# Top-k attention with a squared-ReLU feed-forward: reciprocals of the row sums moved from VectorE to GpSimd, ScalarE's step in another order

## The chip, the core and the metric

The kernel runs on one core of a Trainium2 chip. A core has five engines that run their own instruction streams in order and wait for each other by semaphores: TensorE (PE; its weight loads are listed apart as PEld), VectorE (DVE), ScalarE (ACT), GpSimd (POOL) and SyncE (SP, which here only issues DMAs). The metric is the device time of one execution in microseconds (us).

## What is computed

```python
# q, k, v: (8, 8, 576, 64) float32
scores = (1 / sqrt(64)) * q @ k^T                        # per batch and head, 576 x 576
kth = np.partition(scores, -32, axis=-1)[..., -32:-31]   # 32nd largest of each row
scores = np.where(scores >= kth, scores, -1e9)
attn = exp(scores - max(scores))
attn = attn / (sum(attn) + 1e-9)
x = concat_heads(attn @ v)                               # (4608, 512)
h = np.maximum(x @ w_in, 0.0)                            # w_in (512, 2048)
out = (h * h) @ w_out                                    # w_out (2048, 512)
```

The division by the row sum is the part that the change moves: for each row the kernel needs one reciprocal.

## The kernel before

The 64 pairs of batch and head are taken in twos (`pairs`, 32 of them), and the rows of a pair in chunks of 128. A step `u` (there are `U` = 144, listed in `steps`) handles two such blocks, x = 0 and 1, side by side: 128 rows against all 576 keys, twice. The main loop `for u in range(U)` is a software pipeline written out by hand; `pin` keeps the instructions of each engine in the order in which the program makes them. In one turn of the loop different parts belong to different steps:

- `scores(u + 1)`: TensorE multiplies q and k into two PSUM tiles, `sc_a` and `sc_b` (the two halves of the keys), and ScalarE copies them to SBUF as `s` (L266).
- `pairs_of`, `quads_of`, `both`, `lesser`, `copy_far`: maxima and minima of groups of four scores. VectorE makes the maxima (L282 to L292), GpSimd gets the lesser ones by integer sum and difference (L307, L316), ScalarE copies one tile for it (`most`, L298). The first `EARLY` = 20 steps use a narrower form.
- `topk(u)`: four rounds of VectorE's eight maxima (L342), with the found ones struck out between them (L346). The 32nd value is the bound of the row.
- `drop(u - 1)`: ScalarE negates the row's largest and 32nd value (`neg`, L361); GpSimd compares each score with the bound, once for each x (TENSOR_SCALAR into `gone`, L378), and the result is added to `s` so that dropped scores fall far below zero: by GpSimd itself in the first 20 steps (L380), later by a DMA that GpSimd issues and that adds as it writes (L382).
- `exps(u - 2)`: ScalarE's exponentials into `w_two` (L386); `turn(u - 2)`: SP issues the DMA transpose into `wT`.
- `products(u - 3)`: TensorE multiplies `wT` with v into the one PSUM tile `av_ps`. v carries a column of ones, so that column 64 of the result is the row sum.
- `finish(u - 4)`: `invert` takes the reciprocal of the row sums (`rsum`, VectorE, L436), and `place` multiplies by it on ScalarE while copying to `x_tok` (L452), or to `x_rem` for the steps that hold the last 64 rows of two heads (L459, four instructions instead of two).
- `dense(u, 0)`, `dense(u, 1)`: pieces of the feed-forward part for rows that are ready. An up piece is eight matmuls into a bank `gen`, followed by its `rest`: relu (`rl`, L538) and square (`h`, L544) on ScalarE. A down piece is four matmuls into `dn_ps`; the fourth of a block is followed by a copy (`wide`, L561) and the stores. With `later=True` the `rest` is kept in the list `behind` and run in the next step, behind `topk(u, (0,))` and ahead of `finish`.
- `prepare(u)`: one of the four units that get the next pair ready: q or k transposed by TensorE and copied by ScalarE (`main`, L162), the last rows (`rest`, L199 to L202), and v converted (`values`, L206 and L209). `due(i)` says from which step the units of pair `i` are taken up; `scores(u + 1)` forces what is still missing.
- `w_casts`: the weights converted to bf16 on ScalarE, one piece a step from step 3 on (L624).

So ScalarE's stream in a step of the middle reads: `neg`, the `rest` put off from the step before (relu, square), `x_tok` twice, two score copies, two exps, a preparation if there is one, `most`, v's casts or `wide` if there are any, and a relu and square of the first piece if that was an up piece. GpSimd's reads: two comparisons, the DMA issue, the integer sum, the integer difference.

Of the kernel before, what the change touches and what calls it, by code (L numbers as in the profile page):

```python
# [13 lines left out]
f32 = mybir.dt.float32  # L14
# [3 lines left out]
ALU = mybir.AluOpType  # L18
AF = mybir.ActivationFunctionType
# [4 lines left out]
def kernel(  # L24
# [9 lines left out]
    nc = tc.nc  # L34
# [10 lines left out]
    def pin(ins):  # L45
        tc.keep_in_program_order(ins)
        return ins

    const = ctx.enter_context(tc.tile_pool(name="const", bufs=1))
# [4 lines left out]
    small = fast.enter_context(tc.tile_pool(name="small", bufs=2))  # L54
# [36 lines left out]
    NP = len(pairs)  # L91
# [28 lines left out]
    def fetch(n):  # L120
        while n and fetches:
            fetches.pop(0)[1]()
            n -= 1
# [117 lines left out]
    U = len(steps)  # L241
# [58 lines left out]
    def both(u):  # L300
        d = st[u]
        d["cat"] = scp.tile([128, 2, S], f32, name="cat", bufs=2)
        n_h = 1 if u < EARLY else 2
        wide = n_h * QUAR
        s, less = d["s"], d["cat"][:, :, HALF:HALF + wide].bitcast(i32)
        tt = nc.gpsimd.tensor_tensor
        pin(tt(less, s[:, :, 0:wide].bitcast(i32), s[:, :, HALF:HALF + wide].bitcast(i32), op=ALU.add))  # L307
# [47 lines left out]
    def by_vector(u, x):  # L355
        return u == U - 1 or (u == U - 2 and x == 1)

    def negate(u, ends):
        neg = small.tile([128, 2, 2], f32, name="neg", bufs=4)
        got = st[u]["ends"] if ends == 2 else st[u]["ends"][:, :, 0:1]  # L360
        pin(nc.scalar.activation(neg[:, :, 0:ends], got, AF.Copy, scale=-1.0))  # L361
        return neg
# [7 lines left out]
                e = d["e"][x] = scp.tile([128, S], bf16, name="e", bufs=3)  # L370
                pin(nc.scalar.activation(e[:, :], d["s"][:, x, :], AF.Exp, bias=neg[:, x, 0:1]))

    def drop(u, x):
        d = st[u]
        if x == 0:
            d["neg"] = negate(u, 2)
        s, byte = d["s"], gone[u % 2]
        pin(nc.gpsimd.tensor_scalar(byte[:, x, :, 1], s[:, x, :], scalar1=d["neg"][:, x, 1:2], scalar2=-HUGE, op0=ALU.add, op1=ALU.mult))  # L378
        if by_vector(u, 1) or u < EARLY:
            pin(nc.gpsimd.tensor_tensor(s[:, x, :], s[:, x, :], byte[:, x, :, :].rearrange("p n two -> p (n two)").bitcast(bf16), op=ALU.add))  # L380
        elif x == 1:
            pin(nc.gpsimd.dma_start(out=s[:, :, :].rearrange("p x n -> p (x n)"), in_=byte[:, :, :, :].rearrange("p x n two -> p (x n two)").bitcast(bf16), accum_op=ALU.add))  # L382
# [44 lines left out]
    def sums(u):  # L427
        if u < U - 2:
            return av
        if not last_two:  # L430
            last_two["ps"] = ps_sc.tile([128, 2, 512], f32, name="sc_a")
        return last_two["ps"][:, u - (U - 2), 0:130].rearrange("p (x d) -> p x d", x=2)

    def invert(u):
        r = small.tile([128, 2, 1], f32, name="rsum", bufs=4)
        pin(nc.vector.reciprocal(r[:, :, :], sums(u)[:, :, 64:65]))  # L436
        st[u]["r"] = r

    x_tok = {}
# [4 lines left out]
    def place(u):  # L444
        for x, (i, c, a) in enumerate(steps[u]):
            b, pr = pairs[i]
            o, r = sums(u)[:, x, :], st[u]["r"]
            if c < 4:
                if (b, c) not in x_tok:
                    x_tok[b, c] = ffp.tile([128, 512], bf16, name="x_tok", bufs=8)  # L450
                h = 2 * pr + a
                pin(nc.scalar.activation(x_tok[b, c][:, h * 64:(h + 1) * 64], o[:, 0:64], AF.Copy, scale=r[:, x, :]))  # L452
                left[b, c] = left.get((b, c), 8) - 1
                if left[b, c] == 0:
                    full.append((b, c))
            else:
                for g in range(2):
                    h, rows = 2 * pr + g, slice(64 * g, 64 * g + 64)
                    pin(nc.scalar.activation(x_rem[b % 2][rows, h * 64:(h + 1) * 64], o[rows, 0:64], AF.Copy, scale=r[rows, x, :]))  # L459
                left[b, 4] = left.get((b, 4), 4) - 1  # L460
                if left[b, 4] == 0:
                    soon_moves.append(lambda b=b: rem_unit(b))
        del st[u]
# [35 lines left out]
    def rem_unit(b):  # L499
        tp = ps_one.tile([128, KH, 128], bf16, name="gen", bufs=2)  # L500
        for kh in range(KH):
            pin(nc.tensor.transpose(tp[:, kh, :], x_rem[b % 2][:, kh * 128:(kh + 1) * 128], id_h[:, :]))
        g = b // 2

        def rest():
            for a in range(2):
                rows = slice(64 * a, 64 * a + 64)
                pin(nc.scalar.activation(xt_rem[g % 2][rows, :, (b % 2) * 64:(b % 2 + 1) * 64], tp[rows, :, 64 * a:64 * a + 64], AF.Copy))
            if b % 2:
                rem = xt_rem[g % 2]  # L510
                stores = [[(slice(64 * a, 64 * a + 64), out[(b - 1 + a) * S + 512:(b + a) * S]) for a in range(2)]]
                block(lambda kh: rem[:, kh, :], stores)
        return rest
# [61 lines left out]
    behind = []  # L575

    def piece(later=False):
        turn_of[0] ^= 1
        for q_ in ((ups, downs), (downs, ups))[turn_of[0]]:
            if q_:  # L580
                rest = q_.pop(0)()
                if rest and later:
                    behind.append(rest)
                elif rest:
                    rest()
                return True
        return False

    def dense(u, x, later=False):
        for go in ripe.pop(u, ()):  # L590
            go()
        if moves and x == 1:
            rest = moves.pop(0)()
            if rest and later:
                behind.append(rest)
            elif rest:
                rest()
        if x == 1:
            moves.extend(soon_moves)
            soon_moves.clear()  # L600
        N = 2 if (u >= U - 14 and x == 0) or len(ups) + len(downs) > 24 else 1
        for n in range(N):
            if not piece(later and N == 1) and n == 0 and u < U:
                idle_piece()
# [28 lines left out]
    soon, coming = prep_units(0), 1  # L633
    soon.pop(0)()


    def due(i):
        return first[4 * (i // 4) + 3] - 1 - 4 * (3 - i % 4) if i >= 4 else first[i] - 1

    def prepare(u):  # L640
        nonlocal coming
        if not soon and coming < NP and u >= due(coming) - 4:
            assert coming < 5 or qk_left[coming - 5] == 0
            while fetches and fetches[0][0] <= coming:
                fetch(1)
            soon.extend(prep_units(coming))
            if coming + 1 < NP:
                load_pair(coming + 1)
            coming += 1
        if soon:  # L650
            soon.pop(0)()

    ones = const.tile([128, 1], f32, name="ones")
    pin(nc.gpsimd.memset(ones[:, :], 1.0))
    worst = const.tile([128, 1], f32, name="worst")
# [12 lines left out]
    def ok(w):  # L668
        return 0 <= w < U

    def finish(w):
        if ok(w):
            invert(w)
            place(w)
# [11 lines left out]
    for u in range(U):  # L686
        for x in range(2):
            if ok(u - 1) and not by_vector(u - 1, x):
                drop(u - 1, x)
        quads_of(u)  # L690
        topk(u, (0,))
        while behind:
            behind.pop(0)()
        finish(u - 4)
        if ok(u + 1):
            for i, c, a in steps[u + 1]:
                while coming <= i or (coming == i + 1 and soon):
                    prepare(u)
            scores(u + 1)
            both(u + 1)  # L700
        if ok(u - 2):
            exps(u - 2, 0)
            exps(u - 2, 1)
            turn(u - 2)
        fetch(10 if u < 8 else 3)
        casts_next = bool(soon) and soon[0].__name__ == "values"
        for _ in range(0 if casts_next else 2 if u < 8 else 1):
            prepare(u)
        if u >= Z:
            turn_x(u)  # L710
        topk(u, (1, 2))
        if ok(u + 1):
            pairs_of(u + 1)
            copy_far(u + 1)
            lesser(u + 1)
        topk(u, (3,))
        if casts_next:
            prepare(u)
        if by_vector(u, 1):
            early_exps(u)  # L720
        if u == U - 1:
            exps(u - 1, 0)
        dense(u, 0)
        dense(u, 1, later=8 <= u < U - 1)
        products(u - 3)
        turn_x(u)
        if w_casts and u >= 3:
            w_casts.pop(0)()
        if w_loads and u >= 1:
            w_loads.pop(0)()  # L730
# [163 lines left out]
```

## Time and profile before

| | us |
|---|---|
| Median of 3 runs | 951.43 (948.77 to 954.14) |
| The profiled execution, its own time | 953.31 |
| Its span | 951.5 |
| VectorE busy | 900.3 |
| ScalarE busy | 785.7 |
| GpSimd busy | 775.7 |
| TensorE busy (matmuls) | 690.8 |

In the profile a row of a group reads: line of the program, engine, operation, written tile `<-` read tiles, shapes, number of instructions; busy us and mean ns of one; and the time that the engine stood idle just before them, with what ended it. A row of the timeline reads: start us, duration us, engine, line, operation, tiles, number of merged instructions, and in brackets the idle time before and its releaser. Instructions of one engine overlap a little, so the step from one start to the next can be shorter than a duration.

### The profile page before, as it was taken

How to read it: one execution, taken by the hardware profiler on the slowest of the kernel's cores; microseconds unless marked ns; L12 is line 12 of the kernel's file. 1: busy time of each engine (PE TensorE's matmuls, PEld its weight loads, DVE VectorE, ACT ScalarE, POOL GpSimd, SP SyncE). 2: the span in 40 equal slices, each digit the busy share in tenths (PEclk: the TensorE clock that was granted, in tenths of full speed). 3: DMA queues.
4: the chain of work that ended last, by engine and by line, in shares of the span. 5: the costliest groups of instructions: out<-in, count | busy, mean ns of one | idle time of the engine just before them, and what ended most of it. 6: DMA issues, size and time to landing. Idle time of an engine off the chain costs nothing.

```text
span 951.5 us, 19120 instructions
## 1 busy us (share of the span) xinstructions
PE 690.8 (73%) x5264; PEld 424.4 (45%) x5264; DVE 900.3 (95%) x3635; ACT 785.7 (83%) x1778; POOL 775.7 (82%) x803
## 2 busy tenths in 40 slices
PE   6677767777767777777777777678677776777866
PEld 3333344444444445444444435444444443544544
DVE  5999999999999999999999999899999999899972
ACT  4677797898898879797998878788889877988982
POOL 7888888888888888888888888788888888788840
PEclk9898897988998998989899998987999899799999
DMA  5567766999997998989998899887999989977741
GB/s 138 118 168 160 169 129 132 192 186 208 185 211 160 198 214 185 203 163 197 197 211 177 189 211 171 199 173 166 206 186 200 193 194 203 176 166 164 154 94 43
DMA packets 329969, 166.17 MB, mean 175 GB/s; under 512 B 306560, under 2 KB 306560, under 8 KB 329856
## 3 DMA queue, kind: packets, MB, share of 16 engines
q1 hardware_dynamic: 311088, 92.62, 50.1%
q0 software_dynamic: 17568, 71.97, 33.0%
q8 instruction: 45, 0.74, 0.3%
q14 instruction: 68, 0.56, 0.2%
q10 hardware_dynamic: 1200, 0.30, 0.1%
HBM read 37.75 MB, written 9.44 MB: 50 GB/s over the span
## 4 chain that ended last, share of the span: by engine, by line
DVE 61%; ACT 15%; issue 11%; PE 7%; DMA 3%; SPq 1%; POOL 1%; ACTq 0%; POOLq 0%
DVE m L342 25%; DVE cat L346 16%; DVE sc_b L282 5%; ACT s L266 5%; DVE cat L291 5%; DVE cat L292 5%; DVE most L283 4%; ACT w_two_b L386 2%; PE gen L533 2%; ACT w_two_a L386 2%; PE dn_ps L556 1%; PE sc_a L263 1%; DVE rsum L436 1%; PE sc_b L263 1%; ACT x_tok L452 1%
## 5 line engine op out<-in xcount | busy, mean ns | idle before, releaser
L342 DVE MAX8 m<-cat 128x8 f32<-128x104 f32 (+3 forms) x1152 | 448.2, 432 | 0.0
L346 DVE MATCH_REPLACE8 cat<-m,cat 128x104 f32<-128x104 f32 (+2 forms) x864 | 271.8, 324 | 0.0
L307 POOL TENSOR_TENSOR cat<-s 128x576 int32<-128x576 int32 (+1 forms) x144 | 218.6, 1518 | 17.9 <-ACT s L266 17.0
L316 POOL TENSOR_TENSOR cat<-cat,most 128x576 int32<-128x576 int32 (+1 forms) x144 | 190.0, 1319 | 40.1 <-ACT most L298 24.1
L263 PE MATMUL sc_b<-qkT 64*128 64x288 f32 x512 | 109.1, 495 | 118.8 <-DVE cat L292 55.9
L533 PE MATMUL gen<-xT,w_in 128*128 128x256 bf16 (+1 forms) x1120 | 146.1, 282 | 34.0 <-ACT qkT L162 18.5
L533 PEld LDWEIGHTS <-w_in 128*128 128x128 bf16 x1408 | 127.2, 105 | 86.3 <-issue 56.4
L556 PE MATMUL dn_ps<-w_out,h 128*128 128x512 bf16 x576 | 161.9, 417 | 3.6 <-ACT wide L561 3.6
L263 PE MATMUL sc_a<-qkT 64*128 64x288 f32 x512 | 104.9, 474 | 53.2 <-DVE most L283 28.5
L263 PEld LDWEIGHTS sc_b<-qkT 64*128 64x128 f32 x512 | 49.4, 208 | 166.2 <-ACT neg L361 63.3
L378 POOL TENSOR_SCALAR gone_a<-s,neg 128x576 uint8<-128x576 f32 x143 | 106.7, 746 | 20.4 <-ACT neg L361 9.3
L378 POOL TENSOR_SCALAR gone_b<-s,neg 128x576 uint8<-128x576 f32 x142 | 105.9, 746 | 17.9 <-ACT neg L361 6.8
L452 ACT ACTIVATE x_tok<-av_ps,rsum 128x64 bf16<-128x64 f32 x252 | 64.9, 308 | 58.5 <-DVE rsum L436 58.3
L266 ACT ACTIVATE s<-sc_b 128x576 f32<-128x576 f32 x144 | 94.7, 657 | 7.5 <-PE sc_b L263 7.3
L266 ACT ACTIVATE s<-sc_a 128x576 f32<-128x576 f32 x144 | 93.7, 651 | 5.1 <-PE sc_a L263 4.4
L544 ACT ACTIVATE h<-rl 128x512 bf16<-128x512 f32 x138 | 87.0, 630 | 4.4
L538 ACT ACTIVATE rl<-gen 128x512 f32<-128x512 f32 x142 | 83.8, 590 | 8.0 <-PE gen L533 7.8
L556 PEld LDWEIGHTS <-h 128*128 128x128 bf16 x576 | 55.5, 105 | 70.8 <-issue 33.2
L422 PEld LDWEIGHTS <-wT 128*128 128x128 bf16 (+1 forms) x1600 | 66.4, 105 | 33.1 <-DMA wT<-w_two_c 7.4
L282 DVE TENSOR_TENSOR sc_b<-sc_a,s 128x288 f32<-128x288 f32 x144 | 66.3, 461 | 12.0 <-ACT s L266 9.9
L263 PEld LDWEIGHTS sc_a<-qkT 64*128 64x128 f32 x512 | 44.8, 197 | 65.4 <-ACT w_two_c L386 16.3
L386 ACT ACTIVATE w_two_a<-s,neg 128x576 bf16<-128x576 f32 x96 | 69.6, 783 | 1.8 <-DMA s<-gone_a 1.6
(165 smaller groups left out, 1227.2 us busy)
## 6 DMA issues: line engine op xcount, KB each, us to landing
s<-gone_a POOLq DMA_DIRECT2D x61, 576.0 KB, 4.7
s<-gone_b POOLq DMA_DIRECT2D x61, 576.0 KB, 4.8
v_raw<-in_v_dram SPq DMA_DIRECT2D x64, 128.0 KB, 3.1
out_dram<-wide SPq DMA_DIRECT2D x32, 256.0 KB, 2.7
k_raw<-in_k_dram SPq DMA_DIRECT2D x63, 128.0 KB, 3.1
q_raw<-in_q_dram SPq DMA_DIRECT2D x63, 128.0 KB, 3.3
wide<-in_moe_w_in_dram SPq DMA_DIRECT2D x8, 512.0 KB, 4.2
wide<-in_moe_w_out_dram SPq DMA_DIRECT2D x8, 512.0 KB, 4.0
```

Source lines behind the costliest of these rows:

```text
L263: pin(nc.tensor.matmul(out=ps[j][:, x, 0:HALF], lhsT=lhsT, rhs=rhs, start=True, stop=True))
L266: pin(nc.scalar.activation(s[:, :, j * HALF:(j + 1) * HALF], ps[j][:, :, 0:HALF], AF.Copy))
L282: pin(tt(far, one[:, :, QUAR:HALF], two[:, :, QUAR:HALF], op=ALU.max))
L307: pin(tt(less, s[:, :, 0:wide].bitcast(i32), s[:, :, HALF:HALF + wide].bitcast(i32), op=ALU.add))
L316: pin(tt(less, less, d["most"][:, 0:n_h, :, :].bitcast(i32).rearrange("p h x n -> p x h n"), op=ALU.subtract))
L342: pin(nc.vector.max(out=m[r][:, x, :], in_=part(r, x)))
L346: pin(nc.vector.match_replace(out=part(r, x), in_to_replace=m[r][:, x, :], in_values=part(r, x), imm_value=NEG))
L378: pin(nc.gpsimd.tensor_scalar(byte[:, x, :, 1], s[:, x, :], scalar1=d["neg"][:, x, 1:2], scalar2=-HUGE, op0=ALU.add, op1=ALU.mult))
L386: pin(nc.scalar.activation(w_two[u % 3][:, x, 0:S], d["s"][:, x, :], AF.Exp, bias=d["neg"][:, x, 0:1]))
L533: pin(nc.tensor.matmul(out=hp[:, n * n_rows:(n + 1) * n_rows], lhsT=w_in[:, kh, (f0 + n) * 128:(f0 + n + 1) * 128], rhs=xt(kh), start=(kh ...
L544: pin(nc.scalar.activation(h2, flat, AF.Square))
L556: pin(nc.tensor.matmul(out=op[:, :], lhsT=held["h2"][:, f, c * 128:(c + 1) * 128], rhs=w_out[:, f, :], start=(f == 0), stop=(f == NF - 1)))
```

## The change

Except in the last five steps, the reciprocal is no longer taken by VectorE from PSUM. ScalarE copies the two columns of sums to SBUF (`total`), and GpSimd raises them to the power of -1 with a tensor of minus ones as exponent. `invert(u - 4)` is called from within `drop(u - 1, 1)`, behind the comparison of x = 1 and ahead of the DMA issue (or of the addition, in the first 20 steps). `place(u - 4)` moves behind the score copies and the preparation of the step, and the preparation moves ahead of the exps. The `rest` of the second piece is not put off any more. For the last eight pairs `due` gives fixed steps. ScalarE's stream in a step then reads: `neg`, `total`, two score copies, a preparation, `x_tok` twice, two exps, `most`, casts or `wide`, relu and square. GpSimd's reads: two comparisons, the power, the DMA issue, the integer sum, the integer difference.

```diff
-    def drop(u, x):
+    def drop(u, x, between=None):
         d = st[u]
         if x == 0:
             d["neg"] = negate(u, 2)
         s, byte = d["s"], gone[u % 2]
         pin(nc.gpsimd.tensor_scalar(byte[:, x, :, 1], s[:, x, :], scalar1=d["neg"][:, x, 1:2], scalar2=-HUGE, op0=ALU.add, op1=ALU.mult))
+        if between:
+            between()
         if by_vector(u, 1) or u < EARLY:
...
     def invert(u):
         r = small.tile([128, 2, 1], f32, name="rsum", bufs=4)
-        pin(nc.vector.reciprocal(r[:, :, :], sums(u)[:, :, 64:65]))
+        if u >= U - 5:
+            pin(nc.vector.reciprocal(r[:, :, :], sums(u)[:, :, 64:65]))
+        else:
+            total = small.tile([128, 2, 1], f32, name="total", bufs=4)
+            pin(nc.scalar.activation(total[:, :, :], sums(u)[:, :, 64:65], AF.Copy))
+            pin(nc.gpsimd.tensor_tensor(r[:, :, 0], total[:, :, 0], minus[:, :], op=ALU.pow))
         st[u]["r"] = r
...
     def due(i):
+        if i >= NP - 8:
+            return 101 + 4 * (i - (NP - 8))
         return first[4 * (i // 4) + 3] - 1 - 4 * (3 - i % 4) if i >= 4 else first[i] - 1
...
+    minus = const.tile([128, 2], f32, name="minus")
+    pin(nc.gpsimd.memset(minus[:, :], -1.0))
...
     for u in range(U):
         for x in range(2):
             if ok(u - 1) and not by_vector(u - 1, x):
-                drop(u - 1, x)
+                drop(u - 1, x, (lambda: invert(u - 4)) if x == 1 and ok(u - 4) else None)
         quads_of(u)
         topk(u, (0,))
-        while behind:
-            behind.pop(0)()
-        finish(u - 4)
+        if ok(u - 4) and u == U - 1:
+            invert(u - 4)
         if ok(u + 1):
...
             scores(u + 1)
             both(u + 1)
+        casts_next = bool(soon) and soon[0].__name__ == "values"
+        for _ in range(0 if casts_next else 2 if u < 8 else 1):
+            prepare(u)
+        if ok(u - 4):
+            place(u - 4)
         if ok(u - 2):
             exps(u - 2, 0)
             exps(u - 2, 1)
             turn(u - 2)
         fetch(10 if u < 8 else 3)
-        casts_next = bool(soon) and soon[0].__name__ == "values"
-        for _ in range(0 if casts_next else 2 if u < 8 else 1):
-            prepare(u)
...
         dense(u, 0)
-        dense(u, 1, later=8 <= u < U - 1)
+        dense(u, 1)
         products(u - 3)
```

## The prediction

> **What bounds the kernel now.** Three views, in this order: the engine totals with the groups of instructions, the list of waits, then the order of time. Totals first, and two groups of VectorE (DVE):
>
> ```profile
> span 951.5 us, 19120 instructions
> PE 690.8 (73%) x5264; PEld 424.4 (45%) x5264; DVE 900.3 (95%) x3635; ACT 785.7 (83%) x1778; POOL 775.7 (82%) x803
> ...
> L282 DVE TENSOR_TENSOR sc_b<-sc_a,s 128x288 f32<-128x288 f32 x144 | 66.3, 461 | 12.0 <-ACT s L266 9.9
> ...
> L436 DVE RECIPROCAL rsum<-av_ps 128x2 f32<-128x2 f32 x142 | 23.3, 164 | 7.2 <-PE av_ps L422 7.1
> ```
>
> DVE, 95% busy, sets the pace with its rounds of maxima; its idle time for score copies and sums is 9.9 and 7.1. ScalarE (ACT) and GpSimd (POOL) have a sixth of the span free. ACT's free time is mostly two waits for DVE (total, times, longest):
>
> ```profile
> ACT x_tok L452 <- DVE rsum L436: 58.5, 82, 2.7
> ACT neg L361 <- DVE m L342: 45.6, 69, 2.0
> ```
>
> The pace is read from `neg`, which ACT makes once a step:
>
> ```profile
> 37.38 0.19 ACT L361 ACTIVATE neg<-m 128x4 f32<-128x4 f32 x1
> ...
> 144.29 0.19 ACT L361 ACTIVATE neg<-m 128x4 f32<-128x4 f32 x1
> ...
> 899.19 0.19 ACT L361 ACTIVATE neg<-m 128x4 f32<-128x4 f32 x1
> ```
>
> These are numbers 3, 19 and 140, counted from 0: 16 early steps take 106.9 us (6.68 each), 121 later ones 754.9 (6.24 each), 861.8 together.
>
> **What leaves DVE.** 139 reciprocals of 164 ns, 22.8 us busy. But DVE's instructions overlap, so what counts is start to next start:
>
> ```profile
> 105.81 0.16 DVE L436 RECIPROCAL rsum<-av_ps 128x2 f32<-128x2 f32 x1
> 105.89 0.45 DVE L342 MAX8 m<-cat 128x8 f32<-128x120 f32 x2
> ```
>
> One reciprocal holds DVE back by 0.08 us, 139 of them by 11.1. That is the whole direct gain.
>
> **What goes to ACT.** 139 copies of 128x2 behind `neg`. The nearest row is `neg` itself (128x4, 0.19 to 0.21): 29 us at most, in ACT's idle time, of which these two waits alone are 104.
>
> **What goes to POOL, and the new circle.** This decides. The new order of a step on ACT: neg, the copied sums, two score copies, a preparation if any, place (`x_tok`), two exps, `most`, `wide`, relu and square, next neg. On POOL: two comparisons (TENSOR_SCALAR, they wait for neg), the power, the DMA issue, two integer adds. Place waits for the power, the power stands behind both comparisons, these wait for this step's neg, and neg stands behind all that ACT does after the place before it. The circle closes once a step, whatever DVE does. Its POOL side, in a step where POOL comes free early:
>
> ```profile
> 509.22 0.21 ACT L361 ACTIVATE neg<-m 128x4 f32<-128x4 f32 x1 [1.21 <-DVE m L342]
> ...
> 513.70 0.41 ACT L298 ACTIVATE most<-sc_b 128x288 f32<-128x288 f32 x1
> ```
>
> ```profile
> 509.64 1.56 POOL L378 TENSOR_SCALAR gone_a<-s,neg 128x576 uint8<-128x576 f32 x2
> 511.50 0.89 POOL L382 DMA_DIRECT2D s<-gone_a  x1 [0.30 <-DVE cat L346]
> ...
> 514.24 1.40 POOL L316 TENSOR_TENSOR cat<-cat,most 128x576 int32<-128x576 int32 x1 [0.32 <-ACT most L298]
> 515.74 1.56 POOL L378 TENSOR_SCALAR gone_b<-s,neg 128x576 uint8<-128x576 f32 x2
> ```
>
> Neg to comparison 0.42, the pair 1.56, 0.08 to POOL's next instruction (early rows below), the power p, and a hand-over to ACT that I take as 0.07 (between 0.04, from the end of `rsum` to `x_tok` below, and 0.13, from the end of `most` at 514.11 to 514.24). Place starts 2.13 + p after neg. The DMA issue already idles 0.30 behind the comparisons, so a power of up to about 0.25 delays POOL's own queue by nothing.
>
> ACT's side, start to start. Place and a score copy:
>
> ```profile
> 504.51 0.18 DVE L436 RECIPROCAL rsum<-av_ps 128x2 f32<-128x2 f32 x1
> ...
> 504.73 0.52 ACT L452 ACTIVATE x_tok<-av_ps,rsum 128x64 bf16<-128x64 f32 x2 [0.25 <-DVE rsum L436]
> 505.14 0.65 ACT L266 ACTIVATE s<-sc_a 128x576 f32<-128x576 f32 x1
> ```
>
> and the rest, from five places of the timeline:
>
> ```profile
> 481.81 1.46 ACT L386 ACTIVATE w_two_a<-s,neg 128x576 bf16<-128x576 f32 x2
> 483.14 0.61 ACT L162 ACTIVATE qkT<-gen 128x512 f32<-128x512 f32 x1
> ...
> 496.26 0.60 ACT L538 ACTIVATE rl<-gen 128x512 f32<-128x512 f32 x1
> 496.89 0.63 ACT L544 ACTIVATE h<-rl 128x512 bf16<-128x512 f32 x1
> 497.43 0.19 ACT L361 ACTIVATE neg<-m 128x4 f32<-128x4 f32 x1
> ...
> 516.93 1.28 ACT L459 ACTIVATE x_rem_a<-av_ps,rsum 64x64 bf16<-64x64 f32 x4 [0.25 <-DVE rsum L436]
> ...
> 521.27 0.40 ACT L298 ACTIVATE most<-sc_b 128x288 f32<-128x288 f32 x1
> 521.56 0.59 ACT L561 ACTIVATE wide<-dn_ps 128x512 f32<-128x512 f32 x1
> 522.04 0.21 ACT L361 ACTIVATE neg<-m 128x4 f32<-128x4 f32 x1
> ...
> 538.81 0.62 ACT L206 ACTIVATE vau_c<-v_raw 128x512 bf16<-128x512 f32 x1
> 539.33 0.63 ACT L209 ACTIVATE vau_c<-v_raw 64x128 bf16<-64x128 f32 x2
> ...
> 552.85 0.75 ACT L508 ACTIVATE xt_rem_a<-gen 64x256 bf16<-64x256 bf16 x2
> ```
>
> Place 0.41, the exps 1.33, `most` 0.29, relu with square 1.17, `wide` 0.48, a remainder's four parts 1.28 for place's 0.41, casts of v 1.15, a pair of xt copies 0.75. In 119 steps of the middle the new order holds 122 relus with squares, 31 wides, 25 casts of v, 14 remainders and 6 xt pairs. From place to the next neg ACT needs 0.41 + 1.33 + 0.29 + (122 x 1.17 + 31 x 0.48 + 25 x 1.15 + 14 x 0.87 + 6 x 0.75) / 119 = 3.74, so the circle takes 2.13 + p + 3.74 = 5.87 + p. The preparations lie outside it, in the wait for the power.
>
> A second circle runs through POOL's last add: from the end of `most` 0.13, from add to next comparison 1.50 (514.24 to 515.74), then 1.56, 0.08, p, 0.07, place 0.41, exps 1.33, `most` 0.41: 5.49 + p. In 57 of the 119 steps, the light ones, it is the longer (a plain step has 2.13 + 3.20 = 5.33 + p by the first, one without relu 4.16 + p). Taking the longer one step by step adds 0.22 on average: 6.09 + p.
>
> Early, POOL itself adds the masks, and the power stands behind one such addition too:
>
> ```profile
> 72.09 0.20 ACT L361 ACTIVATE neg<-m 128x4 f32<-128x4 f32 x1
> ```
>
> ```profile
> 74.59 0.75 POOL L378 TENSOR_SCALAR gone_a<-s,neg 128x576 uint8<-128x576 f32 x1
> 75.42 1.28 POOL L380 TENSOR_TENSOR s<-s,gone_a 128x576 f32<-128x576 f32 x1
> ```
>
> ```profile
> L624 ACT ACTIVATE w_in<-wide 128x1024 bf16<-128x1024 f32 x8 | 8.5, 1058 | 0.1
> ```
>
> The power takes the place at 75.42: 3.33 after neg, so 3.40 + p until place. Behind it come place and exps, 1.74, and in the 16 steps 15 casts of weights of 1.06, 3 of v, 2 remainders, 6 relus with squares, an xt pair, a `most`: 3.56 on average. The circle takes 6.96 + p.
>
> **The price p.** This trace has no power. From below: POOL's smallest MEMSET, 0.10. From above: 0.75, a 576-wide comparison. I take 0.32, the smallest two-input row, the nearest in kind:
>
> ```profile
> L352 POOL TENSOR_TENSOR flags<-m 128x36 f32<-128x36 f32 x8 | 2.6, 324 | 0.0
> ...
> L654 POOL MEMSET ones<- 128x1 f32 x1 | 0.1, 103 | 0.1
> ```
>
> The Trainium skill (GPSIMD Engine Reference, 4.1 Engine selection) speaks against the move: it calls two-input elementwise work about twice as slow on GpSimd as on VectorE. An estimate by that page is twice the reciprocal's 0.164, 0.33, and the sum would be 982; no row here has one operation on both engines in one shape, so the trace cannot settle it.
>
> **Other edits.** The second piece's relu is no longer put off: it moves ahead of neg, into the circle, and is counted above. Score copies end at most 0.21 + 0.21 + 0.65 + 0.65 = 1.72 after neg's start. DVE takes them up at
>
> ```profile
> 507.03 0.48 DVE L282 TENSOR_TENSOR sc_b<-sc_a,s 128x288 f32<-128x288 f32 x1
> ```
>
> 3.91 after that step's neg (503.12), so ACT may fall 2.2 behind before DVE waits. This cover is used up once, early. The last eight pairs are spread out from step 97 on, which should end DVE's late stalls; the longer step swallows them. POOL's DMA of the masks starts behind the power:
>
> ```profile
> s<-gone_a POOLq DMA_DIRECT2D x61, 576.0 KB, 4.7
> ```
>
> Issued 2.3 after neg it lands at 7.0; its exps follow in the next step, at about 6.4 + 2.9 = 9.3: nothing. SP issues the transposes behind the exps and then the loads, in the old sequence; products need them a step later, so nothing, and without that cover one more `PE av_ps` wait, 7.1 in all.
>
> **The sum.** Early 16 x 7.28 = 116.5; later 121 x 6.41 = 775.6; 892.1 against 861.8, less the cover of 2.2: +28.1. On the profiled execution's 953.3 (span 951.5; median of the three runs 951.4, so an ordinary one) that gives 981 us. With p = 0.10 it is 137 x 0.22 = 30 less, 951; with 0.75, 59 more, 1040.
>
> **Rivals.**
> - Faster: the circle does not close, because the power is ready when ACT arrives, and DVE stays the bound. Then 11.1 goes, and with earlier score copies and the sums awaited elsewhere up to 9.9 + 7.1: 953.3 - 11.1 - 17.0 = 925. For it: in a step with a preparation of 0.6 ACT reaches place 2 us or more after neg, close to 2.13, and spans on POOL are rough. Against: the comparisons alone are 1.56 behind neg. It holds from the point where place waits less than 0.1 for POOL. Chance 0.25, 925 to 946.
> - No change: p near 0.10, the circle just at the old 6.24: 951. Chance 0.07.
> - A power worked out slowly, 1 us: 137 x 0.68 = 93 more, 1074. Nothing speaks for it but that the operation is new here. Chance 0.12.
> - The forecast, 957 to 1040: 0.56.
>
> Half a per cent, 4.8 us, is about what a measurement of this kernel tells from no change. Faster 0.25, same 0.06, slower 0.69. From 930 (most of the faster case) to 1040 (p = 0.75) about 8 in 10 lie; the likeliest case alone has 951 to 1040.
>
> **What would show it.** Right: in the list of waits x_tok waits for POOL's `rsum`, 0.4 to 0.7 us in nearly every step; DVE's busy share falls below 93%, with idle time at L282 for ACT's `s`; neg follows neg after some 7.3 early and 6.4 later. Wrong: x_tok hardly waits, neg still waits for DVE, and steps fall to 6.02 (6.10 in an undisturbed step now, 509.22 less 503.12, without the 0.08). The power's own mean tells which p held.

## The result, and the profile after

The changed kernel takes 1047.95 us (median of 4 runs, 1047.2 to 1048.18) against 951.01 for the kernel before (4 runs): a ratio of 1.1011, with a 95% interval of 1.0968 to 1.1054. The profiled execution is one of 1048.18 us. The forecast was slower, 981, with a range up to 1040: the side was right, the size was not.

The first lines of the changed kernel's page, the chain (the work that ended last, followed back from the end, with the share of the span that each engine has in it), and the group of the new instruction:

```profile
span 1046.3 us, 18861 instructions
...
PE 730.5 (70%) x5264; PEld 439.0 (42%) x5264; DVE 900.9 (86%) x3496; ACT 795.8 (76%) x1917; POOL 874.3 (84%) x943
...
ACT 37%; POOL 37%; PE 8%; issue 7%; DVE 7%; DMA 3%; SPq 1%; POOLq 0%; ACTq 0%
...
L443 POOL TENSOR_TENSOR rsum<-total,minus 128x2 f32<-128x2 f32 x139 | 99.0, 712 | 11.1
```

The chain of the kernel before, for comparison:

```profile
DVE 61%; ACT 15%; issue 11%; PE 7%; DMA 3%; SPq 1%; POOL 1%; ACTq 0%; POOLq 0%
```

DVE is busy as long as before (900.9 us against 900.3), but in a longer span; it falls from 61% of the chain to 7%, and ACT and POOL share three quarters of it. PE is busy 40 us longer at a lower granted clock (0.874 against 0.911), but it has 8% of the chain after and 7% before. The power takes 712 ns, more than twice the 324 that the sum of the prediction used. The list of waits:

```profile
ACT x_tok L459 <- POOL rsum L443: 143.4, 113, 2.7
...
DVE cat L291 <- ACT most L298: 80.9, 88, 2.7
...
DVE sc_b L282 <- ACT s L266: 26.8, 20, 3.2
```

ACT's wait for VectorE's reciprocals (58.5) has become a wait for GpSimd (143.4, and 16.6 more in the remainders), and DVE, which hardly waited, now waits for ACT. The same three `neg` as before:

```profile
37.61 0.19 ACT L361 ACTIVATE neg<-m 128x4 f32<-128x4 f32 x1
...
158.72 0.19 ACT L361 ACTIVATE neg<-m 128x4 f32<-128x4 f32 x1
...
992.69 0.21 ACT L361 ACTIVATE neg<-m 128x4 f32<-128x4 f32 x1
```

The 16 early steps take 121.1 us (7.57 each instead of 6.68), the 121 later ones 834.0 (6.89 instead of 6.24): 93.3 of the 94.9 us between the two profiled executions. One turn of the circle, first POOL's timeline, then ACT's:

```profile
556.93 1.57 POOL L378 TENSOR_SCALAR gone_b<-s,neg 128x576 uint8<-128x576 f32 x2 [0.91 <-ACT total L442]
558.58 0.71 POOL L443 TENSOR_TENSOR rsum<-total,minus 128x2 f32<-128x2 f32 x1
559.25 0.91 POOL L384 DMA_DIRECT2D s<-gone_b  x1
559.89 1.72 POOL L307 TENSOR_TENSOR cat<-s 128x576 int32<-128x576 int32 x1
561.69 1.40 POOL L316 TENSOR_TENSOR cat<-cat,most 128x576 int32<-128x576 int32 x1
563.19 1.57 POOL L378 TENSOR_SCALAR gone_a<-s,neg 128x576 uint8<-128x576 f32 x2
```

```profile
556.63 0.19 ACT L361 ACTIVATE neg<-m 128x4 f32<-128x4 f32 x1
...
557.32 0.65 ACT L266 ACTIVATE s<-sc_b 128x576 f32<-128x576 f32 x1
559.32 0.52 ACT L459 ACTIVATE x_tok<-av_ps,rsum 128x64 bf16<-128x64 f32 x2 [1.36 <-POOL rsum L443]
...
562.52 0.19 ACT L361 ACTIVATE neg<-m 128x4 f32<-128x4 f32 x1
```

Neg at 556.63, the comparisons at 556.93, the power ends at 559.29, place starts at 559.32, the next neg at 562.52. Then POOL is the late one: its comparisons start only at 563.19, when its adds are done. From 556.93 to 563.19 POOL works without a pause: 6.26 us is what its own queue takes for a step with the power in it.

### The profile page after: what moved, and what is told of

Read it like the earlier page. It is cut to its first block, busy times and chain, and to the rows that moved or that the text cites. A ratio compares the mean times of both kernels' runs of the same rounds, so it can differ in the third digit from the quotient of the medians.

```text
span 1046.3 us, 18861 instructions
## 1 busy us (share of the span) xinstructions
PE 730.5 (70%) x5264; PEld 439.0 (42%) x5264; DVE 900.9 (86%) x3496; ACT 795.8 (76%) x1917; POOL 874.3 (84%) x943
## 4 chain that ended last, share of the span: by engine, by line
ACT 37%; POOL 37%; PE 8%; issue 7%; DVE 7%; DMA 3%; SPq 1%; POOLq 0%; ACTq 0%
POOL gone_a L378 8%; POOL gone_b L378 7%; POOL cat L316 7%; POOL rsum L443 7%; ACT h L551 5%; ACT w_two_b L388 5%; ACT rl L545 5%; ACT w_two_a L388 4%; POOL cat L307 4%; ACT w_two_c L388 4%; ACT x_tok L459 3%; DVE m L342 3%; ACT most L298 3%; POOL s L384 2%; PE gen L540 2%
## 5 line engine op out<-in xcount | busy, mean ns | idle before, releaser
L307 POOL TENSOR_TENSOR cat<-s 128x576 int32<-128x576 int32 (+1 forms) x144 | 228.5, 1587 | 2.5 <-ACT s L266 2.5
L316 POOL TENSOR_TENSOR cat<-cat,most 128x576 int32<-128x576 int32 (+1 forms) x144 | 190.1, 1320 | 25.5 <-ACT most L298 10.8
L263 PE MATMUL sc_b<-qkT 64*128 64x288 f32 x512 | 117.5, 537 | 123.7 <-DVE cat L292 121.5
L459 ACT ACTIVATE x_tok<-av_ps,rsum 128x64 bf16<-128x64 f32 x252 | 65.4, 311 | 145.3 <-POOL rsum L443 143.4
L563 PE MATMUL dn_ps<-w_out,h 128*128 128x512 bf16 x576 | 171.4, 436 | 5.5 <-ACT wide L568 5.5
L540 PEld LDWEIGHTS <-w_in 128*128 128x128 bf16 x1408 | 134.4, 110 | 77.1 <-issue 43.4
L540 PE MATMUL gen<-xT,w_in 128*128 128x256 bf16 (+1 forms) x1120 | 153.3, 293 | 13.9 <-ACT qkT L202 8.4
L291 DVE TENSOR_TENSOR cat<-sc_b,most 128x288 f32<-128x288 f32 x144 | 65.5, 455 | 85.4 <-ACT most L298 80.9
L263 PEld LDWEIGHTS sc_b<-qkT 64*128 64x128 f32 x512 | 52.1, 224 | 174.8 <-issue 110.8
L263 PE MATMUL sc_a<-qkT 64*128 64x288 f32 x512 | 107.6, 500 | 1.6 <-DVE cat L285 1.6
L443 POOL TENSOR_TENSOR rsum<-total,minus 128x2 f32<-128x2 f32 x139 | 99.0, 712 | 11.1
L563 PEld LDWEIGHTS <-h 128*128 128x128 bf16 x576 | 58.2, 109 | 78.8 <-issue 44.1
L282 DVE TENSOR_TENSOR sc_b<-sc_a,s 128x288 f32<-128x288 f32 x144 | 65.8, 457 | 26.8 <-ACT s L266 26.8
```

Source lines behind the costliest of these rows:

```text
L263: pin(nc.tensor.matmul(out=ps[j][:, x, 0:HALF], lhsT=lhsT, rhs=rhs, start=True, stop=True))
L316: pin(tt(less, less, d["most"][:, 0:n_h, :, :].bitcast(i32).rearrange("p h x n -> p x h n"), op=ALU.subtract))
L443: pin(nc.gpsimd.tensor_tensor(r[:, :, 0], total[:, :, 0], minus[:, :], op=ALU.pow))
L540: pin(nc.tensor.matmul(out=hp[:, n * n_rows:(n + 1) * n_rows], lhsT=w_in[:, kh, (f0 + n) * 128:(f0 + n + 1) * 128], rhs=xt(kh), start=(kh ...
L563: pin(nc.tensor.matmul(out=op[:, :], lhsT=held["h2"][:, f, c * 128:(c + 1) * 128], rhs=w_out[:, f, :], start=(f == 0), stop=(f == NF - 1)))
```

## Experiments

The theory: a circle of ACT and POOL (neg, comparisons, power, place, exps, next neg) sets the step, and the power's price decides how long it is. Two rivals: POOL's queue alone has too much work, and place's wait is only its symptom; or ScalarE's new order costs by itself. A time without an interval is that of a single execution; the kernel before took 950 to 955 us beside these runs.

**A cheaper operation in the same place.**

```diff
-            pin(nc.gpsimd.tensor_tensor(r[:, :, 0], total[:, :, 0], minus[:, :], op=ALU.pow))
+            pin(nc.gpsimd.tensor_tensor(r[:, :, 0], total[:, :, 0], minus[:, :], op=ALU.mult))
```

> The power is replaced by a product (the sums are multiplied by -1, so the output is not the reference's); places, order and waits stay. Theory (circle of ACT and POOL through comparisons, power and place, step = 6.09 + p late, 6.96 + p early): a product of two columns takes p of about 0.25 instead of 0.71, so 137 x 0.46 = 63 us less than 1048, about 985; x_tok still waits for POOL. Rival queue (POOL alone has too much work, place's wait is a symptom): POOL's own back-to-back step falls from 6.27 to about 5.8, below DVE's 6.0, and the time falls to about 930. Rival order (ScalarE's new order costs by itself): stays above 1030.

Measured: 983.98 us, the product 195 ns. This is near the circle's 985; with 0.195 instead of the expected 0.25 its own count would be 137 x 0.52 = 71 less, 977. The queue alone would have come down to 930.

**The power kept, but read by nobody.**

```diff
-        if u >= U - 5:
-            pin(nc.vector.reciprocal(r[:, :, :], sums(u)[:, :, 64:65]))
-        else:
+        pin(nc.vector.reciprocal(r[:, :, :], sums(u)[:, :, 64:65]))
+        st[u]["r"] = r
+
+    def unread(u):
+        if u < U - 5:
...
-            pin(nc.gpsimd.tensor_tensor(r[:, :, 0], total[:, :, 0], minus[:, :], op=ALU.pow))
-        st[u]["r"] = r
+            away = small.tile([128, 2, 1], f32, name="away", bufs=1)
+            pin(nc.gpsimd.tensor_tensor(away[:, :, 0], total[:, :, 0], minus[:, :], op=ALU.pow))
...
-                drop(u - 1, x, (lambda: invert(u - 4)) if x == 1 and ok(u - 4) else None)
+                drop(u - 1, x, (lambda: unread(u - 4)) if x == 1 and ok(u - 4) else None)
...
-        if ok(u - 4) and u == U - 1:
+        if ok(u - 4):
             invert(u - 4)
```

> VectorE takes the reciprocals again, in the new order of ScalarE; copy of the sums and power stay on ScalarE and GpSimd in their places, but nothing reads the result. Theory circle: nothing on ACT waits for the power any more, what is left is POOL's own queue, 6.27 a step late and 6.74 early (as back-to-back steps of the changed kernel show), so about 1048 - 121 x 0.62 - 16 x 0.83 = 960. Rival queue: POOL has the same work, so the time stays within 10 of 1048. Rival order: above 1030.

Measured: 993.4 us, between the two. Taking place's wait away gives 55 of the 97 us back; POOL's work alone does not explain 1048, but what is left is more than the queue's 960. Two waits of this run bear on it, the first made by the experiment itself:

```profile
DVE rsum L438 <- ACT total L444: 26.3, 37, 2.0
...
ACT w_two_c L388 <- DMA s<-gone_b: 16.2, 7, 4.6
```

VectorE's reciprocals are listed as waiting for ACT's copy of the same sums, and the exps wait for the DMA of the masks (46.1 in all, by the list of who waited for that DMA), which the changed kernel does not show at all.

**The same with a product**, to see how much of that is the power's time:

```diff
-            pin(nc.gpsimd.tensor_tensor(away[:, :, 0], total[:, :, 0], minus[:, :], op=ALU.pow))
+            pin(nc.gpsimd.tensor_tensor(away[:, :, 0], total[:, :, 0], minus[:, :], op=ALU.mult))
```

> As the run with the unread power (993), with a product in place of the power, also unread. If that run's 51 us over the run with neither (943) are POOL's time for the power (queue of 6.27 a step against DVE's 6.0), they go: 940 to 955, as a product of 0.195 fits into the 0.30 that the DMA issue waits anyway. If they come from the copy of the sums on ACT or from what waits for it, the time stays at 980 to 995.

Measured: 960.89 us. The power's longer time on POOL costs 33 us even where nobody waits for its result. VectorE's wait for the copy is still there (17.4). It is about as much as the 18 us that remain over the next run, though this was not tried by itself.

**New order without the power:** `invert` by VectorE as before, called at its old place.

```diff
-                drop(u - 1, x, (lambda: invert(u - 4)) if x == 1 and ok(u - 4) else None)
+                drop(u - 1, x)
...
-        if ok(u - 4) and u == U - 1:
+        if ok(u - 4):
             invert(u - 4)
```

> New order of ScalarE and the fixed steps of the last pairs, reciprocals by VectorE as before, no copy of sums, no power. Theory circle, and rival queue: DVE is the bound again, late stalls go, 935 to 950. Rival order: above 1000.

Measured: 942.63 us, 0.9901 of the kernel before (0.9863 to 0.9938). The rival of the order falls: the order is not what costs, with the fixed steps it is worth 1%.

**The power ahead of the comparisons.**

```diff
-        if x == 0:
+        if "neg" not in d:
             d["neg"] = negate(u, 2)
...
-                drop(u - 1, x, (lambda: invert(u - 4)) if x == 1 and ok(u - 4) else None)
+                if x == 0 and ok(u - 4) and u < U - 1:
+                    st[u - 1]["neg"] = negate(u - 1, 2)
+                    invert(u - 4)
+                drop(u - 1, x)
```

> The power stands ahead of both comparisons on POOL. Theory circle: the power is ready about 1.1 after neg, place waits at most 0.2 for it; what is left is POOL's queue, now about 6.6 late (the DMA issue waits its 0.30 behind the comparisons again) and 6.74 early: about 1000. Rival queue: same work on POOL, so 1048 or more. Rival order: above 1030 with ACT still waiting little for POOL.

Measured: 1061.28 us, a miss, and what the rival of the queue had forecast (1048 or more). Place's wait went down, but others took over. From the list of waits, and from the view of the masks' DMA (who waited for it, and its time from issue to landing):

```profile
DVE cat L291 <- ACT most L298: 108.2, 60, 6.5
...
ACT x_tok L459 <- POOL rsum L443: 47.2, 57, 2.3
```

```profile
  ACT w_two_c L388: 34.3, 18
  ACT w_two_b L388: 31.4, 13
  ACT w_two_a L388: 17.4, 8
...
DMA to landing us min/median/max: 4.3/5.0/11.2
```

The exps now wait 83 us for the masks, some of which land 11 us after their issue.

**Place moved instead**, behind the exps and `most`, so that they leave the circle:

```diff
-        if ok(u - 4):
-            place(u - 4)
         if ok(u - 2):
             exps(u - 2, 0)
...
             copy_far(u + 1)
             lesser(u + 1)
+        if ok(u - 4):
+            place(u - 4)
         topk(u, (3,))
```

> The changed kernel with nothing but place moved: behind the exps and the copy of the maxima instead of ahead of them. POOL's work, its order and every wait stay. Theory circle: exps and most (1.33 + 0.29) leave the way from the power to the next neg, the circle shrinks to 4.5 + p = 5.2 a step, below POOL's own queue of 6.27, so about what the unread power gave (993): 985 to 1000, and x_tok waits for POOL less than 40 us in all. Rival (POOL's work alone sets the time, or ScalarE's order): within 10 of 1048.

Measured: 1040.44 us, 1.0922 of the kernel before (1.0860 to 1.0983): a miss in time, though the wait went as expected. The time lies within 10 of 1048, where the rival had it. The list of waits, the view of the masks' DMA, the chain, and `neg` number 19 and 140:

```profile
ACT x_tok L459 <- POOL rsum L443: 12.1, 13, 1.5
```

```profile
  ACT w_two_c L388: 59.3, 23
  ACT w_two_b L388: 30.4, 20
  ACT w_two_a L388: 20.9, 12
...
DMA to landing us min/median/max: 4.2/4.9/11.0
```

```profile
DMA 34%; ACT 29%; PE 14%; DVE 12%; issue 5%; POOL 5%; SPq 1%; POOLq 0%; ACTq 0%
```

```profile
149.14 0.19 ACT L361 ACTIVATE neg<-m 128x4 f32<-128x4 f32 x1
...
979.25 0.21 ACT L361 ACTIVATE neg<-m 128x4 f32<-128x4 f32 x1
```

What place no longer waits (143 to 12), the exps wait for the masks (111). The rival's cause does not hold even so: POOL has 5% of the chain, and the 121 later steps take 6.86 us each, where POOL's queue takes 6.26. One of the waits for the masks in order of time:

```profile
568.09 0.95 POOL L384 DMA_DIRECT2D s<-gone_a  x1 [0.17 <-POOL rsum L443]
568.12 1.35 SPq L397 DMA_TRANSPOSE wT<-w_two_b  x1
...
576.10 1.44 ACT L388 ACTIVATE w_two_c<-s,neg 128x576 bf16<-128x576 f32 x2 [4.24 <-DMA s<-gone_a]
576.40 0.10 PEld L424 LDWEIGHTS <-wT 128*128 128x128 bf16 x1 [4.24 <-DMA wT<-w_two_b]
```

POOL's masks and SP's transpose were issued 0.03 us apart, and both took about 8 us. This is no single case. In the run's timeline 9 of the 122 masks' DMAs are issued up to 0.2 us ahead of such a transpose; they land 8.0 to 11.0 us after their issue, 9.3 on average, where the others take 5.2, and 46 of the 111 us stand behind these nine. With the power ahead of the comparisons it is twelve, at 10.0 on average, with 57 of the 83 us behind them. In the changed kernel no masks' DMA is issued so close ahead of a transpose, and none takes more than 6.0.

Was the wait the power's doing, or that of the new place of the exps? The same kernel with the product:

```diff
-            pin(nc.gpsimd.tensor_tensor(r[:, :, 0], total[:, :, 0], minus[:, :], op=ALU.pow))
+            pin(nc.gpsimd.tensor_tensor(r[:, :, 0], total[:, :, 0], minus[:, :], op=ALU.mult))
```

> Place moved behind the exps (1040), with the product of 0.195 in place of the power of 0.712 (the output is not the reference's). If that run stayed slow because the power's own time fills POOL's queue, so that the masks' DMA starts and lands too late for the exps, this falls to 950 to 965 (the unread product gave 961), with the exps waiting less than 20 us in all for the DMA instead of 111. If it stayed slow because exps ahead of place come too early for the DMA whatever POOL does, it stays above 1000 with that wait near 100.

Measured: 950.14 us; the exps wait 27 us for the masks in all, where less than 20 was expected, and

```profile
ACT x_tok L459 <- POOL rsum L443: 1.2, 3, 0.6
```

So the power's length on POOL decides: with place late, 0.52 us less of it a step is worth 90 us. That is more than the 139 x 0.52 = 72 us that POOL saves. One masks' DMA is still issued up to 0.2 us ahead of a transpose (it took 10.0 us) instead of nine, so with the power's length goes how often the two transfers meet; how much of the 90 is due to that and how much to POOL's fuller queue was not told apart. And the run shows the circle by itself: with the short product, moving place from ahead of the exps to behind them takes 34 us off (984 to 950), down to about the time of the same order with the reciprocals on VectorE. That run is the kernel of the new order without the power, with place moved in the same way:

```diff
-        if ok(u - 4):
-            place(u - 4)
...
             lesser(u + 1)
+        if ok(u - 4):
+            place(u - 4)
         topk(u, (3,))
```

> The new order with reciprocals by VectorE (943), place moved in the same way. Nothing waits for POOL there, so theory circle expects no change beyond 0.5%: 939 to 947. If place's position matters for another reason (products waiting for the sums' bank), it is slower: 950 or more.

Measured: 945.67 us, 0.9914 of the kernel before (0.9876 to 0.9952), as expected: the new place costs nothing where nobody waits for POOL.

**The power twice**, the second one read by place:

```diff
+            away = small.tile([128, 2, 1], f32, name="away", bufs=1)
+            pin(nc.gpsimd.tensor_tensor(away[:, :, 0], total[:, :, 0], minus[:, :], op=ALU.pow))
             pin(nc.gpsimd.tensor_tensor(r[:, :, 0], total[:, :, 0], minus[:, :], op=ALU.pow))
```

> The changed kernel with the power taken twice, one after the other, the second one read by place. Theory circle: p doubles from 0.71 to 1.42; the two points so far (984 at 0.195, 1048 at 0.712) give 0.90 us a step for each us of p, so 137 x 0.9 x 0.71 = 88 more, about 1136. If something else set the step by now (DVE's wait for the copied maxima, PE's products), less than half of that: under 1090.

Measured: 1138.59 us. The second power takes 0.687, so 90.4 us for 139 x 0.687 = 95.5: nearly all of POOL's added time is in the total.

**The price by width**, at the start of the run, three of each, added to the kernel of the new order without the power; the first six rows are powers, the last two products:

```diff
+    flat = flags[:, 0:60, :].rearrange("p f n -> p (f n)")
+    pin(nc.gpsimd.memset(flat, 1.5))
+    for op in (ALU.pow, ALU.mult):
+        for w in (1, 2, 4, 8, 16, 32):
+            for again in range(3):
+                pin(nc.gpsimd.tensor_tensor(flat[:, 0:w], flat[:, 80:80 + w], flat[:, 160:160 + w], op=op))
```

> The kernel of the run with reciprocals by VectorE in the new order, with powers and products of 1, 2, 4, 8, 16 and 32 columns on GpSimd at the very start, three of each, over a part of flags that is written later. Only their durations matter. If the power is worked out column by column, its duration grows by about 0.26 us a column (0.71 for two columns against 0.195 for the product), so 32 columns take some 8.5 us and one 0.45; if its price is fixed, all stay near 0.7. The product should grow by 2 to 3 ns a column.

```profile
L664 POOL TENSOR_TENSOR flags<-flags 128x32 f32<-128x32 f32 x3 | 16.3, 5426 | 0.2
L664 POOL TENSOR_TENSOR flags<-flags 128x16 f32<-128x16 f32 x3 | 8.7, 2899 | 0.2
L664 POOL TENSOR_TENSOR flags<-flags 128x8 f32<-128x8 f32 x3 | 4.9, 1636 | 0.2
L664 POOL TENSOR_TENSOR flags<-flags 128x4 f32<-128x4 f32 x3 | 3.0, 1008 | 0.2
L664 POOL TENSOR_TENSOR flags<-flags 128x2 f32<-128x2 f32 x3 | 2.1, 694 | 0.2
L664 POOL TENSOR_TENSOR flags<-flags 128x1 f32<-128x1 f32 x3 | 1.7, 562 | 0.2
...
L664 POOL TENSOR_TENSOR flags<-flags 128x16 f32<-128x16 f32 x3 | 0.7, 219 | 0.2
...
L664 POOL TENSOR_TENSOR flags<-flags 128x2 f32<-128x2 f32 x3 | 0.6, 194 | 0.2
```

From 1 to 32 columns the power grows by (5426 - 562) / 31 = 157 ns a column, over a start of about 400; the product by 25 ns for 14 columns. Neither guess was right (0.26 a column, or a fixed price). The run as a whole took 982.27 us, with the 36 added instructions, some 40 us, at its start.

**What the 1% of the new order comes from**, in one run the order without the fixed steps (taken out of the kernel of the new order), in the other the fixed steps alone (put into the kernel before):

```diff
-        if i >= NP - 8:
-            return 101 + 4 * (i - (NP - 8))
```

> New order of ScalarE with reciprocals by VectorE, but the last eight pairs prepared when they were before. If the fixed steps are what makes the new order faster than before (943 against 951), this is back at 948 to 952; if the order makes it, it stays at 940 to 946. I expect about half and half: 946, since DVE's late stalls for s before the change were 2.49 and 1.53 us.

```diff
     def due(i):
+        if i >= NP - 8:
+            return 101 + 4 * (i - (NP - 8))
```

> The kernel before with nothing changed but the fixed steps of the last eight pairs. By the late stalls of DVE (2.49, 0.43 and 1.53 us between 810 and 835) about 4.5 us less: 947. If the order alone is what helps, 951.

Measured: 949.24 us with the order alone, 0.9945 of the kernel before (0.9916 to 0.9973), and 951.08 with the fixed steps alone, 0.9951 (0.9925 to 0.9977). The kernel before took 954.63 beside these two, so the ratios are what compares with the 0.9901 of both together: about half from each, as far as these intervals can tell.

## Why the prediction was right in kind and wrong in size

- **What leaves DVE**, 0.08 us a step: not contradicted, and never visible, since DVE is no longer the bound.
- **The circle**: right. Place waits for the power behind both comparisons; the product with place early and late (984 and 950) shows that this wait costs time by itself. It is one of two things that cost time, the other is under POOL's queue below.
- **The price p is the step that failed**: "I take 0.32, the smallest two-input row, the nearest in kind". The row was nearest in shape, not in what is worked out; the measured price is 0.712. With it the prediction's own formulas give 16 x (6.96 + 0.71) + 121 x (6.09 + 0.71) = 945.5 instead of 861.8, so 953.3 + 83.7 - 2.2 = 1035. The bound from above, 0.75, did hold the price; the range ended at 1040 all the same, because the formulas are 13 us short.
- **Those 13 us**: 9.6 lie in the steps (early ones took 7.57 against 7.67 by the formula, later ones 6.89 against 6.80), 1.6 outside these 137 steps, and 2.2 are the cover that the sum took off. The cover was read at L282, where DVE takes up `s`; DVE now waits 26.8 us there, but 80.9 at L291 for `most`, which ACT makes behind place. What makes the rest of the tenth in the later steps was not told apart.
- **A floor that the sum left out**: the formulas let the 57 light steps run at 5.49 + p, which with 0.32 is 5.81, less than the 6.02 that the prediction gave DVE. At 0.712 they stand at 6.20 and the floor does not matter. At the product's 0.195 the formulas give 964, where 984 was measured; 57 x 0.33 = 19 us is an estimate of what the floor adds there, and with 0.32 it is 12. No run tries this by itself.
- **The Trainium skill's rule** (GPSIMD Engine Reference, 4.1 Engine selection: about twice as slow, so 0.33 as an estimate): the measurement differs. 712 ns against the 164 of VectorE's reciprocal is 4.3 times. The page's row is on add, mul and max; that the nearest row and the rule agreed was chance, since neither was about a power.
- **POOL's queue and the masks**: the prediction said that up to 0.25 of power costs the queue nothing. That holds (the product fits, 950), but it drew no conclusion for a longer one. At 0.71 the queue takes 6.26 a step, more than the 6.02 that it gave for DVE. The masks' DMA it put at nothing: "its exps follow in the next step". In the changed kernel that holds, no exps are listed as waiting for it; once the exps no longer stand behind place's wait, they wait 111 us. The two limits hide each other: moving place alone gives 8 us, shortening the operation alone 64, both 98.
- **The other rivals**: "faster" would have needed place to wait less than 0.1; it waits 1.3 where it waits. "A power worked out slowly, 1 us", 1074, was the nearest in kind, and got 0.12. **Fixed last pairs**: by themselves they are worth half a per cent; that the longer step swallows them, as the prediction said, no run shows.

## What to carry to other kernels

Before moving a small operation to an idle engine, measure that operation on that engine: a row of equal shape says little about a function that has to be worked out. Then follow the result all the way round: if its reader stands ahead of the work that releases its producer, the two engines form a circle, and free time on either does not help; the reader belongs behind work that does not need it. And when a wait goes without the time going, read the chain again: here it had passed to a transfer that is issued behind the same instruction.

## What the runs showed of the hardware

A power on GpSimd took about 0.40 us plus 0.157 for each column of 128 values, from 1 to 32 columns; a product 0.19 with almost nothing for each column (0.219 at 16). The masks' DMA has a median of 4.5 to 5.0 us from issue to landing. Issued up to 0.2 us ahead of SP's transpose of the exps it took 8.0 to 11.0 (nine times with place late) and 7.8 to 11.2 (twelve times with the power ahead of the comparisons), 5.7 to 10.8 with the unread power (eight times), and the transpose about as long; with place late, those issued 0.3 to 1 us ahead took 4.9 on average. So the two seem to hold each other up when they start together; no run changed their distance alone.
